# Sliding-window attention block with a SiLU feed-forward: from pool-scheduled stages to one hand-ordered stream, with projections beside attention, four-head score bursts, masks on GpSimd and reused SBUF regions

## The chip, the core and the metric

The kernel runs on one core of one Trainium2 chip. The core has TensorE (PE: matmuls and transposes, with weight loads shown apart as PEld), VectorE (DVE), ScalarE (ACT), GpSimd (POOL), SyncE (SP, which here only issues transfers) and 16 DMA engines. The metric is the device time of one execution in microseconds (us).

## What is computed

Input `x` is 2048 rows of 1024 bf16 numbers. The reference, cut to what matters:

```
def _A_ref(x, wqkv, wo):
    B, S, D = x.shape
    H = 32; Dh = D // H; W = 256
    qkv = (x @ wqkv) ...
    scores = jnp.einsum("bhqd,bhkd->bhqk", q, k) * (Dh ** -0.5)
    mask = (idx[:, None] - idx[None, :] >= 0) & (idx[:, None] - idx[None, :] < W)
    p = _softmax(jnp.where(mask[None, None], scores, -1e9), axis=-1)
    o = jnp.einsum("bhqk,bhkd->bhqd", p, v)
    return o ... @ wo
h = x + _A_ref(_layernorm(x), A_wqkv, A_wo)
h2 = h + einsum(silu(einsum(_layernorm(h), B_w1)), B_w2)      # B_w1: 1024 x 3584
```

There are 32 heads of 32 numbers. A query sees itself and the 255 rows before it, so a tile of 128 queries meets three tiles of 128 keys: its own (upper-triangular mask), the one before (no mask) and the one before that (mask on the other side).

## The kernel before

Rows are worked in 16 tiles of 128, four tiles to a block of 512 (b = 0 to 3). There are three stages, one after the other, each with its own tile pools; inside a stage a scheduler orders the instructions of each engine by dependencies and buffers.

1. Projections (lines 133 to 163). For each block: load x (L126), layernorm on DVE (statistics L45 and L46, reciprocal root by four Newton steps L28 to L31, normalization L52), transposes on PE (L143) copied out by DVE (L144), then 24 dense groups of eight 128x512 matmuls: 16 for q and k (L150), 8 for v (L159). ACT copies each group out of PSUM (L152, L162). A column of ones beside v (VW = 33) gives the softmax sums.
2. Attention (lines 184 to 238), one query tile at a time. For each pair of heads, six score matmuls (L200: 32 rows of the array, 128 columns) write `sc`; ACT takes the exponential (L207) into `eT`; DVE multiplies two of the three 128-wide pieces by masks (L209, L210); six matmuls with 33 columns (L216) add up `o_ps`; DVE divides (L221, L222). When a query tile's 32 heads are done, `o_sb` is transposed (L228, L230), projected by `wo` in 16 matmuls of 512 columns (L235, one PSUM buffer, `misc`), added to x (L237) and written to `h_dram` (L238). `w1` (7.3 MB) is loaded on POOL's queue and `wo` (2 MB) on SP's once the projections have freed their space (L170, L178); `x_t` (L187) stands behind `wo`.
3. Feed-forward (lines 254 to 284). For each block: reload h (L256), layernorm, transposes (L263, L264), 28 groups of eight matmuls with `w1` (L269), tanh on ACT (L272) and the product on DVE (L273) for SiLU, then 8 groups of 28 matmuls with `w2` (L280), residual (L282) and output (L284). `w2` (7.3 MB) is loaded on POOL's queue after the attention stage has freed its space (L246).

Of the kernel before, what the change touches and what calls it, by code (L numbers as in the profile page):

```python
# [9 lines left out]
F32 = mybir.dt.float32  # L10
# [10 lines left out]
def _rsqrt_newton(nc, pool, v_ap, out_ap, shape, tagp):  # L21
    vi = v_ap.bitcast(I32)
    yi = out_ap.bitcast(I32)
    nc.vector.tensor_scalar(out=yi, in0=vi, scalar1=1, scalar2=None, op0=ALU.logical_shift_right)
    nc.vector.tensor_scalar(out=yi, in0=yi, scalar1=-1, scalar2=0x5F3759DF, op0=ALU.mult, op1=ALU.add)
    t = pool.tile(shape, F32, name=f"rsq_t_{tagp}", tag=f"rsq_t_{tagp}")
    for _ in range(4):
        nc.vector.tensor_tensor(out=t, in0=out_ap, in1=out_ap, op=ALU.mult)  # L28
        nc.vector.tensor_tensor(out=t, in0=t, in1=v_ap, op=ALU.mult)
        nc.vector.tensor_scalar(out=t, in0=t, scalar1=-0.5, scalar2=1.5, op0=ALU.mult, op1=ALU.add)  # L30
        nc.vector.tensor_tensor(out=out_ap, in0=out_ap, in1=t, op=ALU.mult)  # L31


def _layernorm_block(nc, small, xb, ln, nj, D, tagp):
    FMAX = nc.vector.BN_STATS_FMAX
    nch = (D + FMAX - 1) // FMAX
    SD = nc.vector.BN_STATS_DIM
    AD = nc.vector.BN_AGGR_DIM
    stats = small.tile([P, nj, nch, SD], F32, name=f"ln_stats_{tagp}", tag=f"ln_stats_{tagp}")
    mv = small.tile([P, nj, AD], F32, name=f"ln_mv_{tagp}", tag=f"ln_mv_{tagp}")  # L40
    for j in range(nj):
        for c in range(nch):
            lo = c * FMAX
            hi = min(D, lo + FMAX)
            nc.vector.bn_stats(out=stats[:, j, c, :], in_=xb[:, j, lo:hi])  # L45
        nc.vector.bn_aggr(out=mv[:, j, :], in_=stats[:, j, :, :])  # L46
    var = small.tile([P, nj], F32, name=f"ln_var_{tagp}", tag=f"ln_var_{tagp}")
    nc.vector.tensor_scalar(out=var, in0=mv[:, :, 1], scalar1=LN_EPS, scalar2=None, op0=ALU.add)
    rstd = small.tile([P, nj], F32, name=f"ln_rstd_{tagp}", tag=f"ln_rstd_{tagp}")
# [9 lines left out]
def kernel(  # L59
# [15 lines left out]
    F = B_w1.shape[1]  # L75
    H = N_HEADS
    DH = D // H
    assert DH == 32 and D % P == 0 and S % 512 == 0 and F % P == 0
    NT = S // P
    KT = D // P  # L80
    FT = F // P
# [233 lines left out]
```

## Time and profile before

| what | value |
|---|---|
| timed runs | 963.44, 964.41, 967.6 us; median 964.41 |
| span of the profiled execution | 960.9 us; its own time is not given beside it, the median lies 3.5 us above the span |
| busy | PE 890.9 us (93%), DVE 370.4 (39%), ACT 311.7 (32%), POOL 13.1 (1%) |
| moved | 44.95 MB by DMA, mean 47 GB/s |
| mean granted TensorE clock | 0.865 of full |

The span is the time from the first to the last instruction on the core. The chain of work that ended last is followed back from the last instruction, at each step to what released it; an "issue" row in it is time in which an engine waited for nothing that the profile shows. Busy time on PE is occupancy: it does not say how fast the array was clocked. That stands in its own column, PEclk, 1.00 for full speed. A row of the timeline gives start, duration, engine, line, operation, output<-input, shape, count, and in brackets the idle time before it with what ended it.

### The profile page before, as it was taken

What the parts mean: (1) busy time and instruction counts of PE and PEld (TensorE: products, weight loads), DVE (VectorE), ACT (ScalarE), POOL (GpSimd) and SP (SyncE); (2) the same over time, 40 slices, a digit from 0 to 9 for tenths busy, and PEclk for the clock granted to TensorE, in tenths of its full rate; (3) what the DMA queues carried; (4) which work ended last, traced back from release to release, by engine and by line L of the source; (5) the groups of instructions that cost most, each with busy time, mean ns of one, the idle gap of its engine ahead of it and who ended that gap; (6) DMA issues with size and microseconds to landing.
All of it is one profiled execution on the core that took longest, in us unless ns stands there. A gap on an engine that the chain in (4) does not pass through costs nothing.

```text
span 960.9 us, 14267 instructions
## 1 busy us (share of the span) xinstructions
PE 890.9 (93%) x6012; PEld 448.8 (47%) x6080; DVE 370.4 (39%) x1112; ACT 311.7 (32%) x465; POOL 13.1 (1%) x26
## 2 busy tenths in 40 slices
PE   3999999968999999999999399999999999999998
PEld 2454444434555555555555144444444444444443
DVE  5940100034555545545555753215521463123311
ACT  0323333343655655555565023101310032003200
POOL 1000000010000000000000200000000000000000
PEclk9999999956766666667676689999999999999999
DMA  9200000091100000000100550001000200000000
GB/s 365 72 1 1 1 1 1 1 370 69 38 30 23 23 24 23 24 23 23 34 34 13 196 209 1 12 23 55 1 1 23 65 1 1 23 23 1 1 23 22
DMA packets 16559, 44.95 MB, mean 47 GB/s; under 512 B 1392, under 2 KB 1392, under 8 KB 16496
## 3 DMA queue, kind: packets, MB, share of 16 engines
q1 hardware_dynamic: 13440, 29.36, 8.6%
q0 software_dynamic: 3056, 14.68, 4.0%
q8 instruction: 47, 0.77, 0.3%
q14 instruction: 16, 0.13, 0.0%
HBM read 35.65 MB, written 8.39 MB: 46 GB/s over the span
## 4 chain that ended last, share of the span: by engine, by line
PE 81%; issue 8%; DVE 4%; DMA 3%; ACT 3%; SPq 0%; ACTq 0%; DVEq 0%
PE h L269 20%; PE acc L280 20%; PE sc L200 12%; PE acc L150 12%; PE o_ps L216 7%; PE acc L159 6%; PE acc_o L235 3%; ACT eT L207 3%; DMA x_t<-in_A_x_dram 2%; PE tpo L228 1%; DVE ln_stats_b L45 1%; DVE ln2T L264 1%; PE tp L143 1%; DMA x_blk<-in_A_x_dram 1%; DVE ln_stats_a L45 0%
## 5 line engine op out<-in xcount | busy, mean ns | idle before, releaser
L207 ACT ACTIVATE eT<-sc 128x768 bf16<-128x768 f32 (+2 forms) x256 | 187.6, 769 | 150.1 <-issue 65.5
L269 PE MATMUL h<-ln2T,w_sb 128*128 128x512 bf16 x876 | 194.8, 381 | 4.4 <-DVE ln2T L264 3.1
L280 PE MATMUL acc<-w_sb,gT 128*128 128x512 bf16 x880 | 193.2, 379 | 0.8
L272 ACT ACTIVATE th<-h 128x512 f32<-128x512 f32 x112 | 66.9, 597 | 311.2 <-PE h L269 304.5
L200 PE MATMUL sc<-qT_all,kT_all 32*128 32x128 bf16 x1440 | 159.9, 268 | 3.5 <-ACT eT L207 1.4
L269 PEld LDWEIGHTS <-w_sb 128*128 128x128 bf16 x896 | 88.1, 98 | 110.0 <-issue 6.2
L280 PEld LDWEIGHTS <-gT 128*128 128x128 bf16 x896 | 87.7, 98 | 105.7
L273 DVE SCALAR_TENSOR_TENSOR gT<-th,h 128x512 bf16<-128x512 f32 x112 | 76.8, 686 | 101.9 <-ACT th L272 101.8
L150 PE MATMUL acc<-lnT,wqkv_sb 128*128 128x512 bf16 x500 | 110.6, 379 | 2.5 <-DVE lnT L144 1.7
L216 PE MATMUL o_ps<-v_aug,eT 128*128 128x33 bf16 x1440 | 110.2, 192 | 1.8 <-DVE eT L209 0.6
L216 PEld LDWEIGHTS <-eT 128*128 128x128 bf16 x1440 | 72.6, 105 | 66.4 <-issue 22.9
L235 PE MATMUL acc_o<-wo_sb,oT 128*128 128x512 bf16 x240 | 85.1, 497 | 15.0 <-DMA wo_sb<-in_A_wo_dram 7.5
L210 DVE TENSOR_TENSOR eT<-eT,maskU 128x256 bf16<-128x256 bf16 x256 | 72.0, 282 | 47.9 <-ACT eT L207 47.5
L282 DVE SCALAR_TENSOR_TENSOR o_t<-acc,hb 128x512 bf16<-128x512 f32 x32 | 22.1, 692 | 168.8 <-PE acc L280 154.6
L200 PEld LDWEIGHTS <-kT_all 32*128 32x128 bf16 x1440 | 72.0, 105 | 28.6 <-issue 10.4
L209 DVE TENSOR_TENSOR eT<-eT,maskL 128x256 bf16<-128x256 bf16 x224 | 63.8, 285 | 49.7 <-ACT eT L207 48.9
L150 PEld LDWEIGHTS <-wqkv_sb 128*128 128x128 bf16 x512 | 49.8, 98 | 62.0 <-DVE lnT L144 1.6
L159 PE MATMUL acc<-wqkv_sb,lnT 128*128 128x512 bf16 x252 | 55.7, 379 | 0.2
L235 PEld LDWEIGHTS <-oT 128*128 128x128 bf16 x256 | 28.4, 120 | 55.1 <-issue 39.8
L237 DVE TENSOR_TENSOR h_t<-acc_o,x_t 128x512 bf16<-128x512 f32 x32 | 22.1, 692 | 61.7 <-PE acc_o L235 48.8
L144 DVE COPY lnT<-tp 128x1024 bf16<-128x1024 bf16 x16 | 10.2, 685 | 89.2 <-PE tp L143 89.2
L152 ACT CAST qT_all<-acc 128x512 bf16<-128x512 f32 x32 | 18.7, 586 | 64.9 <-PE acc L150 64.9
(47 smaller groups left out, 296.4 us busy)
## 6 DMA issues: line engine op xcount, KB each, us to landing
w_sb<-in_B_w_dram POOLq DMA_DIRECT2D x8, 896.0 KB, 15.1
w_sb<-in_B_w_dram POOLq DMA_DIRECT2D x7, 1024.0 KB, 11.8
wqkv_sb<-in_A_wqkv_dram SPq DMA_DIRECT2D x8, 768.0 KB, 11.1
x_blk<-in_A_x_dram SPq DMA_DIRECT2D x4, 1024.0 KB, 7.3
x_t<-in_A_x_dram SPq DMA_DIRECT2D x16, 256.0 KB, 2.8
h_dram<-h_t SPq DMA_DIRECT2D x16, 256.0 KB, 2.0
hb<-h_dram SPq DMA_DIRECT2D x4, 1024.0 KB, 5.9
out_dram<-o_t SPq DMA_DIRECT2D x16, 256.0 KB, 2.0
```

The lines of the kernel that those rows point to most:

```text
L150: nc.tensor.matmul(acc[:], lhsT=wqkv_sb[:, kt, col0:col0 + P], rhs=lnT[:, kt, :], start=(kt == 0), stop=(kt == KT - 1))
L159: nc.tensor.matmul(acc[:], lhsT=lnT[:, kt, j * P:(j + 1) * P], rhs=wqkv_sb[:, kt, col0:col0 + 512], start=(kt == 0), stop=(kt == KT - 1))
L200: nc.tensor.matmul(sc[:, hh, j * P:(j + 1) * P], lhsT=kT_all[r0:r0 + DH, g, kt * P:(kt + 1) * P], rhs=qT_all[r0:r0 + DH, g, qt * P:(qt + 1 ...
L207: nc.scalar.activation(out=eT[:, :, jlo * P:3 * P], in_=sc[:, :, jlo * P:3 * P], func=ACT.Exp, scale=scale)
L209: nc.vector.tensor_tensor(out=eT[:, :, 0:P], in0=eT[:, :, 0:P], in1=maskL_b, op=ALU.mult)
L210: nc.vector.tensor_tensor(out=eT[:, :, 2 * P:3 * P], in0=eT[:, :, 2 * P:3 * P], in1=maskU_b, op=ALU.mult)
L216: nc.tensor.matmul(o_ps[:, hl, 0:VW], lhsT=eT[:, hh, j * P:(j + 1) * P], rhs=v_aug[:, kt, h, :], start=(j == jlo), stop=(j == 2),)
L235: nc.tensor.matmul(acc[:], lhsT=oT[:, kt, :], rhs=wo_sb[:, kt, c * 512:(c + 1) * 512], start=(kt == 0), stop=(kt == KT - 1))
L269: nc.tensor.matmul(h1[:], lhsT=w1_sb[:, kt, ft * P:(ft + 1) * P], rhs=lnT[:, kt, :], start=(kt == 0), stop=(kt == KT - 1))
L272: nc.scalar.activation(out=th[:], in_=h1[:], func=ACT.Tanh, scale=0.5)
L273: nc.vector.scalar_tensor_tensor(out=gT[:, ft, :], in0=th[:], scalar=1.0, in1=h1[:], op0=ALU.add, op1=ALU.mult)
L280: nc.tensor.matmul(acc[:], lhsT=gT[:, ft, j * P:(j + 1) * P], rhs=w2_sb[:, ft, c * 512:(c + 1) * 512], start=(ft == 0), stop=(ft == FT - 1))
```

## The change

The whole program is written in one order by hand (`tc.manual_schedule()`), without pools for the large tiles: six SBUF regions are made once and viewed at fixed offsets by everything that uses them over time (`r_w` holds first wqkv, then w1; `r_t` the transposed layernorm of odd blocks, then residual tiles; `r_o` the x tiles, then wo; `r_a` q, k, v, later the gated activations, most of w2, and h of block 0; `r_e` the exponentials, later h and its transpose).

- Block 0 is projected first, tile by tile. Then, for b = 1 to 3, each of the 24 dense groups of block b follows a score burst of block b-1. The 24 bursts of block 3 stand beside the `wo` groups of blocks 0 to 2; block 3's `wo` groups stand inside the first feed-forward block.
- A burst (`scores`) covers 4 heads at once and 512 queries in three kinds A, B, C (`PIECES`): two matmuls per head, 512 columns in all, the four heads in the four row groups of the array and in four PSUM banks. Two exponentials of 128x1024 follow on ACT.
- Masks are applied in place by GpSimd's `affine_select`, not by DVE's multiplications.
- The 24 + 24 value matmuls of a head group, then its four transposes, are put behind the dense groups of the next head group's three bursts (`pending`, `tail_of`). Layernorm steps of the next block are dealt out one per burst (`steps`).
- PSUM evictions of dense groups beside attention are on DVE. 14 matmuls on zeros open the PE stream. All loads are issued by SP, w1 in 8 pieces at the end of the projections, w2 in 7 pieces into slots as they come free.

On PE, before, in the middle of the attention stage (`o_ps` values, `sc` scores, `eT` exponentials, `kT_all` keys):

```order
L216 MATMUL o_ps<-v_aug,eT 128x33
L200 LDWEIGHTS kT_all
L200 MATMUL sc<-qT_all,kT_all 128x128
L200 LDWEIGHTS kT_all
L200 MATMUL sc<-qT_all,kT_all 128x128
L216 LDWEIGHTS eT
L216 MATMUL o_ps<-v_aug,eT 128x33
```

On PE, after, the end of a dense group of block b and the value matmuls behind it (`r_w` weights, `r_t` activations, `r_e` exponentials, `r_a` v; the bracket names the engine waited for):

```order
L193 LDWEIGHTS r_t
L193 MATMUL acc_83<-r_w,r_t 128x512
L265 LDWEIGHTS r_e [waits Pool_49]
L265 MATMUL o_ps<-r_a,r_e 128x33
L265 LDWEIGHTS r_e
L265 MATMUL o_ps<-r_a,r_e 128x33
```

What moved: attention's small matmuls stood among themselves; now each run of them stands behind eight 512-column matmuls, and they wait for POOL where they waited for DVE.

On SP, before, from the end of the projections into attention (w1 is on POOL's queue):

```order
L126 DMA x_blk<-in_A_x_dram 128x4x1024 x3
L178 DMA wo_sb<-in_A_wo_dram 128x1024 x8
L187 DMA x_t<-in_A_x_dram 128x1024 x2
L238 DMA h_dram<-h_t 128x1024
L187 DMA x_t<-in_A_x_dram 128x1024
```

On SP, after, from the projections of block 3 into its attention (`in_B_w_dram` is w1; L206 is `load_res`, the residual tiles of the `wo` groups):

```order
L345 DMA r_o<-in_A_wo_dram 128x4x1024
L346 DMA r_o<-in_A_wo_dram 128x4x1024
L363 DMA r_w<-in_B_w_dram 128x3584 x8
L206 DMA r_t<-in_A_x_dram 128x1024 x2
L216 DMA h_dram<-r_t 128x1024
L206 DMA r_t<-in_A_x_dram 128x1024
```

What moved: wo is loaded a block earlier, and the first residual tiles now stand behind the eight pieces of w1 on the one queue that issues everything.

On DVE, before, in the attention stage:

```order
L237 TENSOR_TENSOR h_t<-acc_o,x_t 128x512
L209 TENSOR_TENSOR eT<-eT,maskL 128x2x128
L210 TENSOR_TENSOR eT<-eT,maskU 128x2x128
L209 TENSOR_TENSOR eT<-eT,maskL 128x2x128
L210 TENSOR_TENSOR eT<-eT,maskU 128x2x128
```

On DVE, after, where block 3's attention begins (`acc_82`, `acc_83` dense groups, L213 the addition of a residual tile):

```order
L203 CAST r_a<-acc_82 128x512
L283 COPY r_a<-tp_ps 128x512
L213 TENSOR_TENSOR r_t<-acc_83,r_t 128x512
L272 RECIPROCAL recip<-o_ps 128x8
L273 TENSOR_TENSOR r_n<-o_ps,recip 128x4x64
L213 TENSOR_TENSOR r_t<-acc_82,r_t 128x512
```

What moved: the mask products are gone from DVE and evictions of dense groups have come; the division of the previous head group stands behind the first residual addition.

The diff, cut to its core:

```diff
+PIECES = {
+    "A": [(0, 0, 3, 0), (-2, 0, 1, 3)],
+    "B": [(-1, 0, 2, 0), (2, 2, 2, 2)],
+    "C": [(3, 3, 1, 0), (1, 1, 3, 1)],
+}
+CHUNKS = [
+    [(-2, "A", 3), (-1, "B", 0), (0, "A", 0)],
+    [(-1, "B", 1), (0, "A", 1), (1, "C", 1)],
+    [(0, "A", 2), (1, "C", 2), (2, "B", 2)],
+    [(1, "C", 3), (2, "B", 3), (3, "C", 0)],
+]
+KINDS = "ABC"
...
+    h_dram = dram.tile([S, D], BF16, name="h_dram")
+    r_w = big.tile([P, 28672], BF16, name="r_w")
+    r_t = big.tile([P, 4096], BF16, name="r_t")
+    r_o = big.tile([P, 8192], BF16, name="r_o")
...
+    r_e = big.tile([P, 12288], BF16, name="r_e")
+    r_n = big.tile([P, 1536], BF16, name="r_n")
+    sc = [ps.tile([P, 2, 512], F32, name=f"sc{i}") for i in range(2)]
...
+    wqkv = view(r_w, 0, KT, 3 * D)
+    w1 = view(r_w, 0, KT, F)
+    lnT_b = [view(r_w, 24576, KT, 512), view(r_t, 0, KT, 512)]
+    x_ring = [view(r_o, i * 1024, 1024) for i in range(8)]
+    wo = view(r_o, 0, KT, D)
+    t_in = [view(r_t, i * 1024, 1024) for i in range(2)]
+    t_out = [view(r_t, 2048 + i * 1024, 1024) for i in range(2)]
+    qT = [view(r_a, (4096, 8192, 12288, 0)[b], G, 512) for b in range(NB)]
+    kT = [view(r_a, 16384 + 4096 * b, G, 512) for b in range(NB)]
+    v = view(r_a, 32768, S // P, H, VW)
+    gT = view(r_a, 4096, FT, 512)
+    W2_SLOT = (0, 1, 2, 3, 6, 4, 5)
+    w2_off = 18432
+    w2 = [view(r_a, w2_off + 4096 * s, 4, D) for s in W2_SLOT]
+    ebuf = [view(r_e, 1024 * i, 2, 512) for i in range(12)]
+    h_blk = [view(r_a, w2_off + 4096 * 4, 4, D)] + [view(r_e, 8192, 4, D)] * 3
+    ln2T = [view(r_a, w2_off + 4096 * 5, KT, 512), view(r_e, 0, KT, 512), view(r_e, 4096, KT, 512), view(r_e, 0, KT, 512)]
+    wqkv_v = A_wqkv.rearrange("(kt p) n -> p kt n", p=P)
+    wo_v = A_wo.rearrange("(kt p) n -> p kt n", p=P)
+    w1_v = B_w1.rearrange("(kt p) f -> p kt f", p=P)
+    w2_v = B_w2.rearrange("(ft p) n -> p ft n", p=P)
...
-    for b in range(NB):
-        xb = x_blks.pop(b)
-        if b + 1 < NB:
-            load_x_blk(b + 1)
-        ln = lnp.tile([P, 4, D], BF16, name="ln1", tag="ln1")
-        _layernorm_block(nc, small, xb, ln, 4, D, "a")
-        lnT = lnp.tile([P, KT, 512], BF16, name="lnT", tag="lnT")
...
-        for g in range(G):
-            for which, dst in ((0, qT_all), (1, kT_all)):
-                col0 = which * D + g * P
-                acc = psA1.tile([P, 512], F32, name="acc", tag="acc")
-                for kt in range(KT):
-                    nc.tensor.matmul(acc[:], lhsT=wqkv_sb[:, kt, col0:col0 + P], rhs=lnT[:, kt, :],
-                                     start=(kt == 0), stop=(kt == KT - 1))
-                nc.scalar.copy(out=dst[:, g, b * 512:(b + 1) * 512], in_=acc[:])
...
-    for qt in range(NT):
...
-                sc = psA2.tile([P, 2, 512], F32, name="sc", tag="sc")
...
-                eT = ework.tile([P, 2, 3 * P], BF16, name="eT", tag="eT")
-                nc.scalar.activation(out=eT[:, :, jlo * P:3 * P], in_=sc[:, :, jlo * P:3 * P], func=ACT.Exp, scale=scale)
-                if jlo == 0:
-                    nc.vector.tensor_tensor(out=eT[:, :, 0:P], in0=eT[:, :, 0:P], in1=maskL_b, op=ALU.mult)
-                nc.vector.tensor_tensor(out=eT[:, :, 2 * P:3 * P], in0=eT[:, :, 2 * P:3 * P], in1=maskU_b, op=ALU.mult)
...
+    def load_x(b, j):
+        nc.sync.dma_start(out=x_ring[(b % 2) * 4 + j], in_=x2d[(b * 4 + j) * P:(b * 4 + j + 1) * P, :])
+    def load_wqkv(c0):
+        nc.sync.dma_start(out=wqkv[:, :, c0:c0 + 512], in_=wqkv_v[:, :, c0:c0 + 512])
+    load_x(0, 0)
+    load_wqkv(2 * D)
+    load_x(0, 1)
+    load_wqkv(2 * D + 512)
+    load_x(0, 2)
+    load_x(0, 3)
+    for c0 in (0, D, 512, D + 512):
+        load_wqkv(c0)
+    make_identity(nc, ident[:])
+    warm = ebuf[0]
+    nc.vector.memset(warm, 0.0)
+    nc.gpsimd.memset(v[:, :, :, DH:VW], 1.0)
+    for i in range(14):
+        nc.tensor.matmul(sc[0][:, i % 2, :], lhsT=warm[:, 0, 0:P], rhs=warm[:, 0, :], start=True, stop=True)
...
+    def load_res(b, j, src):
+        nc.sync.dma_start(out=t_in[j % 2], in_=src[(b * 4 + j) * P:(b * 4 + j + 1) * P, :])
+    def wo_group(b, j, c):
+        acc = next_acc()
+        for g in range(G):
+            nc.tensor.matmul(acc, lhsT=qT[b][:, g, j * P:(j + 1) * P], rhs=wo[:, g, c * 512:(c + 1) * 512],
+                             start=(g == 0), stop=(g == G - 1))
+        nc.vector.tensor_tensor(out=t_out[j % 2][:, c * 512:(c + 1) * 512], in0=acc,
+                                in1=t_in[j % 2][:, c * 512:(c + 1) * 512], op=ALU.add)
+        if c == 1:
+            nc.sync.dma_start(out=h_dram[(b * 4 + j) * P:(b * 4 + j + 1) * P, :], in_=t_out[j % 2])
...
+    def scores(b, g, kind):
+        for kt, q0, nq, ch in PIECES[kind]:
+            t = b * 4 + kt
+            if t < 0:
+                continue
+            for hh in range(4):
+                r0 = hh * DH
+                nc.tensor.matmul(
+                    sc[hh // 2][:, hh % 2, ch * P:(ch + nq) * P],
+                    lhsT=kT[t // 4][r0:r0 + DH, g, (t % 4) * P:(t % 4 + 1) * P],
+                    rhs=qT[b][r0:r0 + DH, g, q0 * P:(q0 + nq) * P],
+                    start=True, stop=True, tile_position=(r0, 0),
+                )
+        lo, hi = 0, 512
...
+            e = e_of(b * G + g, kind, pair)
+            nc.scalar.activation(out=e[:, :, lo:hi], in_=sc[pair][:, :, lo:hi], func=ACT.Exp, scale=scale)
+            if kind == "A":
+                mask(e, 0, 1, True)
+                mask(e, 2, 1 if b == 0 else 2, False)
+            elif kind == "B":
+                if b > 0:
...
+    def mask(e, c0, n, upper):
+        ap = e[:, :, c0 * P:(c0 + n) * P].rearrange("p h (c q) -> p h c q", q=P)
+        sgn = 1 if upper else -1
+        nc.gpsimd.affine_select(out=ap, in_=ap, pattern=[[0, 2], [0, n], [sgn, P]],
+                                compare_op=ALU.is_ge if upper else ALU.is_gt,
+                                fill=0.0, base=0, channel_multiplier=-sgn)
...
+    def attn_out(b, g, pair):
+        i = b * G + g
+        for qt in range(4):
+            for hh in range(2):
+                chunks = [x for x in CHUNKS[qt] if b * 4 + x[0] >= 0]
+                for n, (kt, kind, ch) in enumerate(chunks):
+                    nc.tensor.matmul(
+                        o_ps[:, qt * 2 + hh, 0:VW],
+                        lhsT=e_of(i, kind, pair)[:, hh, ch * P:(ch + 1) * P],
+                        rhs=v[:, b * 4 + kt, g * 4 + pair * 2 + hh, :],
+                        start=(n == 0), stop=(n == len(chunks) - 1),
+                    )
...
+    def attn_transpose(b, g):
+        i = b * G + g
+        for qt in range(4):
+            nc.tensor.transpose(out=tp_ps[:, qt * P:(qt + 1) * P], in_=obuf[i % 3][:, qt, :], identity=ident[:])
+        nc.vector.tensor_copy(out=qT[b][:, g, :], in_=tp_ps[:, 0:512])
...
+    def tail_of(b, g):
+        return [lambda: attn_out(b, g, 0), lambda: attn_out(b, g, 1), lambda: attn_transpose(b, g)]
...
+    for b in range(1, NB):
+        dense = [lambda j=j, c=c: v_group(b, j, c, dve) for j in range(4) for c in range(2)]
+        dense += [lambda w=w, g=g: qk_group(b, w, g, dve) for g in range(G) for w in range(2)]
+        if b + 1 < NB:
+            for j in range(4):
...
+        else:
+            steps = []
+            nc.sync.dma_start(out=wo[:, 0:4, :], in_=wo_v[:, 0:4, :])
+            nc.sync.dma_start(out=wo[:, 4:8, :], in_=wo_v[:, 4:8, :])
+        n = 0
+        for g in range(G):
+            for kind in KINDS:
+                scores(b - 1, g, kind)
+                dense[n]()
+                if pending:
+                    pending.pop(0)()
+                if steps and n >= 4 and n % 3 != 2:
+                    steps.pop(0)()
+                n += 1
+            pending = tail_of(b - 1, g)
+        while steps:
+            steps.pop(0)()
...
+    for kt in range(KT):
+        nc.sync.dma_start(out=w1[:, kt, :], in_=w1_v[:, kt, :])
...
+    load_res(0, 0, x2d)
...
+    for g in range(G):
+        for kind in KINDS:
+            scores(NB - 1, g, kind)
+            b, j, c = dense[n]
...
+            wo_group(b, j, c)
+            if pending:
+                pending.pop(0)()
+            if n == 9:
+                steps = ln2_steps(0)
+                nc.sync.dma_start(out=w2[0], in_=w2_v[:, 0:4, :])
+            if steps and n >= 9:
+                steps.pop(0)()
+            n += 1
+        pending = tail_of(NB - 1, g)
+    while steps:
...
+    for b in range(NB):
+        extra = []
+        if b == 0:
+            extra = [(f, 1) for f in pending]
+            pending = []
+        for ft in range(FT):
+            acc = h1_group(b, ft)
+            if extra:
+                extra.pop(0)[0]()
+                if not extra and b == 0:
+                    for i in (1, 2, 3, 4):
+                        load_w2(i)
+            silu(b, acc, ft)
...
+        if b == 0:
+            load_w2(6)
+        steps = ln2_steps(b + 1) if b + 1 < NB else []
+        load_res(b, 0, h_dram)
...
+                nc.vector.scalar_tensor_tensor(out=t_out[j % 2][:, c * 512:(c + 1) * 512], in0=acc, scalar=0.5,
+                                               in1=t_in[j % 2][:, c * 512:(c + 1) * 512], op0=ALU.mult, op1=ALU.add)
...
+        while steps:
+            steps.pop(0)()
```

357 lines of the change are left out of this document (169 added, 188 removed).

## The prediction

> **What bounds the kernel now.** The span first, then the windows by stage, then the chain of waits.
>
> ```profile
> span 960.9 us, 14267 instructions
> ```
>
> The windows view gives busy time per engine, then PEclk, DMA share and GB/s; three windows are the middles of stages, four are looks at one place.
>
> ```profile
> 130.00:180.00 50.00, 48.85 (x235) 22.67 (x239) 1.29 (x2) 16.40 (x28) 0.00 (x0) 1.00 0.00 0
> 206.00:210.00 4.00, 2.04 (x5) 0.60 (x4) 0.57 (x2) 0.45 (x1) 0.00 (x0) 0.50 1.03 409
> 224.00:225.00 1.00, 0.64 (x16) 0.35 (x12) 0.97 (x3) 0.59 (x2) 0.00 (x0) 1.00 0.00 0
> 323.00:324.00 1.00, 1.00 (x29) 0.79 (x27) 0.53 (x1) 0.00 (x0) 0.00 (x0) 1.00 0.00 0
> 330.00:331.00 1.00, 1.00 (x16) 0.66 (x13) 0.98 (x5) 0.79 (x2) 0.00 (x0) 0.50 0.00 0
> 340.00:420.00 80.00, 76.28 (x791) 43.34 (x796) 42.43 (x158) 44.38 (x59) 0.00 (x0) 0.67 0.09 28
> 580.00:650.00 70.00, 69.63 (x319) 31.75 (x325) 15.99 (x24) 10.15 (x17) 0.00 (x0) 1.00 0.03 12
> ```
>
> Projections (130 to 180) and feed-forward (580 to 650) keep PE at full clock, without gaps. Attention (340 to 420) shows PE just as busy, at a mean clock of 0.67: 1.00 at 323, 0.50 at 330. It is the slow stage, with the two seams beside it. The chain in order of time (start, length, what) dates them:
>
> ```profile
> 56.35 5.34 PE acc L159 x24
> ...
> 197.11 22.43 DMA x_t<-in_A_x_dram
> ...
> 321.74 4.61 issue
> ...
> 343.08 5.52 issue
> ...
> 557.60 1.44 PE h L269 x3
> ...
> 660.30 10.74 PE h L269 x49
> 671.09 10.74 PE h L269 x49
> ...
> 760.52 10.74 PE h L269 x49
> ```
>
> Block 0 is projected by 61.7; the chain then waits 22.43 us for `x_t`, queued behind weights; one query tile takes 343.08 - 321.74 = 21.3 us; feed-forward starts at 557.6 and one block of it takes 100.2 us. 49 shown matmuls (one record is missing) and the next start give 10.79 / 50 = 0.216 us per dense matmul, 1.73 per group of eight; 448 of them are 96.7, so 3.5 us per feed-forward block are its layernorm seam.
>
> **Block 0, after.** The layernorm of the first block before:
>
> ```profile
> 6.11 1.88 DVE L45 BATCH_NORM_STATS2 ln_stats_a<-x_blk 128x6 f32<-128x512 bf16 x3 [6.11 <-DMA x_blk<-in_A_x_dram]
> ...
> 11.44 0.17 DVE L48 TENSOR_SCALAR ln_var_a<-ln_mv_a 128x4 f32<-128x4 f32 x1
> ...
> 15.23 1.92 DVE L52 TENSOR_SCALAR ln<-x_blk,ln_mv_a,ln_rstd_a 128x1024 bf16<-128x1024 bf16 x4
> ```
>
> A megabyte lands at 6.1; a quarter of it comes 0.75 MB / 409 GB/s = 1.9 earlier, at 4.2. One tile's layernorm: two statistics of 0.63 and the aggregate, 1.4; 15 small steps (19 took 3.79 above, 0.2 each), 3.0; normalization 0.48; so 9.1. Then each of four tiles costs PE two dense groups, 3.45, and about 1.9 for its transposes and ACT's copy behind two evictions, in which PE waits: 4 x 5.35 = 21.4, to 30.5. Sixteen q and k groups are 27.6; the next block's 32 transposes, a quarter of a dense matmul each, 1.7, and a wait on the one transpose buffer, 1. Total **61**, as before: nothing gained. The zero matmuls lie under the load.
>
> **One burst.** The terms at full clock, from the timeline:
>
> ```profile
> 217.99 1.09 ACT L207 ACTIVATE eT<-sc 128x512 bf16<-128x512 f32 x2 [11.54 <-PE sc L200]
> ```
>
> ```profile
> 224.07 0.30 PE L200 MATMUL sc<-qT_all,kT_all 32*128 32x128 bf16 x8
> ```
>
> ```profile
> 323.06 0.82 PEld L216 LDWEIGHTS <-eT 128*128 128x128 bf16 x22
> ```
>
> ```profile
> 338.02 2.27 ACT L207 ACTIVATE eT<-sc 128x768 bf16<-128x768 f32 x3 [1.23 <-PE sc L200]
> ```
>
> - Scores: eight matmuls over the four row groups stood in 0.30 us (clock 1.00 at 224), where one after another at 0.054 each they would need 0.43; so row groups run together. A burst streams 512 columns per head: 0.216 when four run together, 0.86 when none do. I take 0.3.
> - Dense group: 1.73.
> - Value matmuls: 22 weight loads in 0.82, 0.034 each (clock 1.00 at 323): 24 take 0.82. Kind C has four transposes in their place, 0.22.
> - ACT: 0.757 for 768 columns, 0.545 for 512, so 0.97 for 1024, two per burst. Behind the second, the next scores and their flight to ACT, 0.5: a floor of 2.45.
> - Changing between sorts of matmul and their semaphores: 0.15, an estimate (bounds 0 and 0.4).
>
> A and B: 0.3 + 1.73 + 0.82 + 0.15 = 3.0, PE's. C: PE needs 2.25, ACT's 2.45 decides. Mean **2.82**; 72 bursts, 203. In block 0 a query tile has fewer keys (18 value matmuls for 24): 24 bursts at 2.6, 62. Transposes of three layernorms, 5. Together **270**. It replaces the projections of blocks 1 to 3, sixteen query tiles and both seams, 61.7 to 557.6, 496 us in all, but for what stands below.
>
> DVE per three bursts: three evictions, two divisions and a transpose copy, none above 0.69 by the rows here, and 1.7 of layernorm (13.3 us a block, worked out like the first tile's, over eight head groups): under 5.9 of 8.45 us, not the bound.
>
> ```profile
> L237 DVE TENSOR_TENSOR h_t<-acc_o,x_t 128x512 bf16<-128x512 f32 x32 | 22.1, 692 | 61.7 <-PE acc_o L235 48.8
> L144 DVE COPY lnT<-tp 128x1024 bf16<-128x1024 bf16 x16 | 10.2, 685 | 89.2 <-PE tp L143 89.2
> ```
>
> POOL's timeline shows three selects and a memset, no mask of the new sizes:
>
> ```profile
> 1.19 0.28 POOL masks.py:199 TENSOR_SCALAR_AFFINE_SELECT ident<-ident 128x128 bf16<-128x128 bf16 x1
> 1.43 0.28 POOL L96 TENSOR_SCALAR_AFFINE_SELECT maskU<-maskU 128x128 bf16<-128x128 bf16 x1
> 1.67 0.20 POOL L98 MEMSET maskL<- 128x128 bf16 x1
> ...
> 3.73 0.49 POOL L99 TENSOR_SCALAR_AFFINE_SELECT maskL<-maskL 128x128 bf16<-128x128 bf16 x1
> ```
>
> A head group's masks are 12 selects over 4096 columns. Start to start, 0.24 per 128 columns: 1.9 ns a column, 7.7 us, under the 8.45 of three bursts. By the spans it is 9.1 (0.28) to 15.6 (0.49). I take 7.7, the two rows that stand undisturbed; the last select starts while another POOL instruction runs. [...]
>
> **The seam into block 3's attention.** w1's eight pieces wait for block 3's last dense groups, since they reuse `r_w`, and `load_res(0,0)` stands behind them on SP. 7.34 MB at 409 GB/s are 18, with the residual tile and landing about 20. DVE reaches the first residual addition after 2 us (scores and a dense group) and stops there, in order; the divisions of the last head group of block 2 are queued behind it, so `o_ps` stays taken. PE runs that burst, the next scores and dense group, 5 us in all, and waits at its second run of value matmuls until 21: 16. The clock falls to 0.50 in such a gap (window 206 to 210, same wait before) and costs about 2 on return. **18.** The `x_t` wait above is its like. Behind it, `hb` of block 0 lands behind 1 MB of w2: 1.
>
> **Feed-forward and end.**
>
> ```profile
> 957.20 0.69 DVE L282 SCALAR_TENSOR_TENSOR o_t<-acc,hb 128x512 bf16<-128x512 f32 x1 [5.35 <-PE acc L280]
> ```
>
> 1792 dense matmuls, 386.7; the 64 of block 3's `wo`, 13.8; value matmuls and transposes of the last head group, 2; three layernorms' transposes, 5 (their DVE work now lies under 48 us of matmuls); the last w2 piece, issued only when the first `w1` half is done, 1. **409.** After the last eviction starts, 3.7 as now.
>
> Sum: 61 + 270 + 18 + 1 + 409 + 3.7 = 762.7 of span, and 3.5 around it (964.41 - 960.9): **766 us**.
>
> **The rivals.**
>
> 1. POOL binds. At 0.28 per 128 columns and 0.2, an estimate, for each of six waits on ACT a head group takes 10.3 instead of 8.45; PE then waits at each first run of value matmuls. 24 head groups: +44, block 0 +2: 812. For it: the spans on POOL. Against it: the starts 0.24 apart. Chance 0.18.
> 2. No wait at w1: the residual tiles land among w1's pieces, or DVE's stop is covered: 748. Against it: `x_t` now, 22.43 us. Chance 0.08.
> 3. The clock falls in the bursts. One row holds full clock while dense matmuls ran:
>
> ```profile
> 324.22 1.89 PE L235 MATMUL acc_o<-wo_sb,oT 128*128 128x512 bf16 x8
> ```
>
>    They end at 326.1, and the clock is at 0.50 at 330, with PE shown fully busy by small matmuls. So small matmuls do not hold it; whether 1.73 dense us in every 2.82 do, no row shows. I think so: no stretch of 3 us is without them. At half clock a burst is 3.45 + 0.6 + 1.2 + 0.15 = 5.4, kind C 4.5, mean 5.1; 72 x 5.1 + 24 x 4.8 + 10 = 492 for 270: 988, slower than before. It needs nine in ten bursts at half clock to lose, (964 - 766) / 222. Half of them give 877. Chances 0.03 for all, 0.09 for part. [...]
>
> **How the numbers follow.** Forecast 0.60, POOL 0.18, no wait 0.08, part of the bursts slow 0.09, all slow 0.03, unnamed 0.02. The forecast's own bounds: 0.25 more or 0.15 less per burst is 24 or -14, scores one after another 0.56 x 96 = 54 at worst: 750 to 800. The range takes in no wait and POOL, 738 to 825. Within 0.5% is about what a measurement of this kernel tells from no change. Faster 0.95, same 0.01, slower 0.04.
>
> **What would show it.** Right: PEclk 1.00 through the bursts but for one gap; a burst every 2.8 us; a wait of 15 to 20 us for `r_t` by DMA at L213, with PE behind it; no "<-POOL" among PE's larger waits; feed-forward blocks of 98.5. Wrong: PE waiting for POOL at L265 in every head group (rival 1), PEclk near 0.5 beside dense groups (rival 3), PE waiting for ACT in all kinds (scores not together).

## The result, and the profile after

The changed kernel takes 845.37 us, the median of four runs (844.29 to 846.42), beside 966.0 for the kernel before (963.44 to 967.65): a ratio of 0.876, 95% interval 0.8737 to 0.8783. The forecast was 766 us, so the sign is right, but the time is 79 us above the forecast and lies above the range (738 to 825) too. The profiled execution took 846.29 us. The first lines of the profile's page give the span, the busy time of each engine and the row of the granted clock over the span:

```profile
span 844.6 us, 12753 instructions
...
PE 724.2 (86%) x5265; PEld 353.4 (42%) x5358; DVE 329.5 (39%) x738; ACT 257.1 (30%) x325; POOL 171.6 (20%) x375
...
PEclk9999999999996989999999999999999999999999
```

PE is now at full clock nearly everywhere, but busy for 86% of the span instead of 93%: time is lost in gaps, not to the clock. Three rows of the timeline date the stages: the first score burst, the first feed-forward group, the last eviction.

```profile
60.12 0.34 PE L229 MATMUL sc<-r_a 32*128 32x384 bf16 x4
...
347.40 1.89 PE L402 MATMUL acc<-r_a,r_w 128*128 128x512 bf16 x8
...
841.03 0.69 DVE L446 SCALAR_TENSOR_TENSOR r_t<-sc,r_t 128x512 bf16<-128x512 f32 x1 [5.35 <-PE sc L444]
```

Set beside the terms of the sum (all us; bursts are 270 with the w1 seam's 18 and 1 for `hb`):

| stage | predicted | after |
|---|---|---|
| block 0's projections | 61 | 60.1 |
| 96 bursts with the seam | 289 | 287.3 |
| feed-forward to the last eviction | 409 | 493.6 |
| end | 3.7 | 3.6 |
| around the span | 3.5 | 1.7 |

Everything ahead of the feed-forward came as forecast, and the feed-forward is 85 us too long. (The term around the span was 1.8 too large: 964.41 was set against the span of another execution, and in the runs that have both, time and span differ by 1.7.) Before, PE ran the feed-forward almost without a gap (69.63 of 70 us busy). The windows view (PE, PEld, DVE, ACT, POOL busy, then PEclk, DMA share, GB/s) shows where PE now stands idle, first in the bursts, then at the seam, then in one feed-forward block:

```profile
61.00:250.00 189.00, 183.47 (x2189) 101.34 (x2222) 107.52 (x253) 126.87 (x142) 121.44 (x267) 1.00 0.04 13
250.00:272.00 22.00, 7.43 (x84) 3.81 (x82) 1.92 (x5) 5.82 (x6) 6.28 (x14) 0.74 0.89 357
...
485.00:608.00 123.00, 102.28 (x473) 46.28 (x483) 37.86 (x72) 16.72 (x28) 0.00 (x0) 0.99 0.08 26
```

The bursts keep PE busy for 97% at clock 1.00. The feed-forward window has the clock too, 0.99, and yet PE is idle for 20.7 of its 123 us. The list of PE's waits (waiting instruction, what it waited for: us in total, times, longest) names them:

```profile
PE sc L402 <- DVE r_a L412: 47.4, 33, 1.5
PE o_ps L265 <- DVE r_n L273: 18.6, 2, 16.6
PE sc L444 <- DVE r_t L446: 13.3, 8, 3.2
...
PE sc L402 <- DVE r_t L213: 4.9, 6, 1.0
...
PE acc L211 <- DVE r_t L213: 4.3, 1, 4.3
...
PE sc L402 <- DVE r_t L446: 2.4, 3, 0.8
```

The second row is the w1 seam. In the first, third, fourth and last, matmuls that write `sc` in the feed-forward wait for DVE. The timeline of one such wait:

```profile
489.47 0.60 ACT L411 ACTIVATE r_a<-sc 128x512 f32<-128x512 f32 x1 [1.13 <-PE sc L402]
490.10 0.69 DVE L412 SCALAR_TENSOR_TENSOR r_a<-r_a,sc 128x512 bf16<-128x512 f32 x1 [1.04 <-ACT r_a L411]
490.84 1.89 PE L402 MATMUL sc<-r_e,r_w 128*128 128x512 bf16 x8 [1.41 <-DVE r_a L412]
```

A group ends in one bank of `sc` at 489.4 (a bank is here the 128x512 f32 numbers that one group writes). Before the next group may start in the other bank, tanh (0.60) and the product (0.69) of the group just finished have to be through: PE stands for 1.41 us. In the feed-forward the banks follow one another as `acc0`, `acc1`, then the first and second half of `sc0`, then those of `sc1`. The second half of each waits; that is two waits in six groups. The chain shows what six groups then take:

```profile
485.80 3.64 PE sc L402 x16
...
499.31 3.63 PE sc L402 x16
```

13.51 us, where six groups without a wait would be 6 x 1.73 = 10.4 (10.36 in e1, below). Half of 13.51 - 10.36 is 1.58: so much a wait costs, 0.17 more than its idle time.

### The profile page after: what moved, and what is told of

Its sections match the earlier page's. It is cut to its first block, busy times and chain, and to the rows that moved or that the text cites. A ratio compares the mean times of both kernels' runs of the same rounds, so it can differ in the third digit from the quotient of the medians.

```text
span 844.6 us, 12753 instructions
## 1 busy us (share of the span) xinstructions
PE 724.2 (86%) x5265; PEld 353.4 (42%) x5358; DVE 329.5 (39%) x738; ACT 257.1 (30%) x325; POOL 171.6 (20%) x375
## 4 chain that ended last, share of the span: by engine, by line
PE 77%; DVE 10%; DMA 8%; ACT 3%; issue 2%; SPq 0%; ACTq 0%; DVEq 0%
PE sc L402 15%; PE sc L444 13%; PE acc L201 12%; PE acc L444 8%; PE acc L402 7%; PE acc L193 7%; PE acc L211 4%; PE o_ps L265 4%; PE sc L229 3%; DMA r_t<-in_A_x_dram 3%; DVE r_a L412 3%; DMA r_e<-h_dram 2%; ACT r_a L411 2%; DVE r_t L446 2%; PE tp_ps L173 1%
## 5 line engine op out<-in xcount | busy, mean ns | idle before, releaser
L240 ACT ACTIVATE r_e<-sc 128x1024 bf16<-128x1024 f32 (+2 forms) x192 | 175.8, 967 | 112.7 <-PE sc L229 112.7
L255 POOL TENSOR_SCALAR_AFFINE_SELECT r_e<-r_e 128x256 bf16<-128x256 bf16 (+1 forms) x368 | 168.6, 487 | 176.4 <-ACT r_e L240 172.5
L402 PEld LDWEIGHTS <-r_w 128*128 128x128 bf16 x896 | 87.1, 97 | 166.3 <-issue 65.0
L402 PE MATMUL sc<-r_e,r_w 128*128 128x512 bf16 x452 | 105.0, 379 | 41.4 <-DVE r_a L412 38.8
L444 PEld LDWEIGHTS <-r_a 128*128 128x128 bf16 x896 | 88.1, 99 | 121.9 <-issue 20.5
L444 PE MATMUL sc<-r_a 128*128 128x512 bf16 x548 | 125.9, 386 | 13.9 <-DVE r_t L446 13.3
L444 PE MATMUL acc<-r_a 128*128 128x512 bf16 x327 | 73.7, 379 | 1.0 <-DMA r_a<-in_B_w_dram 0.6
L201 PEld LDWEIGHTS <-r_w 128*128 128x128 bf16 x512 | 46.1, 98 | 59.4 <-issue 10.3
L265 PE MATMUL o_ps<-r_a,r_e 128*128 128x33 bf16 x1440 | 46.4, 178 | 18.6 <-DVE r_n L273 18.6
L201 PE MATMUL acc<-r_t,r_w 128*128 128x512 bf16 x240 | 58.0, 380 | 3.0 <-issue 1.7
L265 PEld LDWEIGHTS <-r_e 128*128 128x128 bf16 x1440 | 45.9, 96 | 34.3 <-issue 19.7
L201 PE MATMUL acc<-r_w 128*128 128x512 bf16 x244 | 57.0, 379 | 1.7 <-issue 0.9
L211 PE MATMUL acc<-r_o,r_a 128*128 128x512 bf16 x195 | 51.5, 404 | 5.9 <-DVE r_t L213 4.3
L412 DVE SCALAR_TENSOR_TENSOR r_a<-r_n,sc 128x512 bf16<-128x512 f32 x30 | 20.6, 688 | 78.3 <-ACT r_n L411 78.3
L402 PE MATMUL acc<-r_e,r_w 128*128 128x512 bf16 x208 | 48.6, 379 | 0.4
L402 PE MATMUL sc<-r_a,r_w 128*128 128x512 bf16 x139 | 33.4, 378 | 13.7 <-DVE r_a L412 8.6
L229 PE MATMUL sc<-r_a 32*128 32x128 bf16 (+2 forms) x704 | 40.5, 279 | 0.0
L211 PEld LDWEIGHTS <-r_a 128*128 128x128 bf16 x256 | 24.0, 101 | 36.9 <-issue 14.2
L213 DVE TENSOR_TENSOR r_t<-acc,r_t 128x512 bf16<-128x512 f32 x26 | 17.8, 685 | 45.1 <-PE acc L211 25.3
```

What stands on the lines that cost most here:

```text
L201: nc.tensor.matmul(acc, lhsT=wqkv[:, kt, col0:col0 + P], rhs=lnT_b[b % 2][:, kt, :], start=(kt == 0), stop=(kt == KT - 1))
L211: nc.tensor.matmul(acc, lhsT=qT[b][:, g, j * P:(j + 1) * P], rhs=wo[:, g, c * 512:(c + 1) * 512], start=(g == 0), stop=(g == G - 1))
L229: nc.tensor.matmul(sc[hh // 2][:, hh % 2, ch * P:(ch + nq) * P], lhsT=kT[t // 4][r0:r0 + DH, g, (t % 4) * P:(t % 4 + 1) * P], rhs=qT[b][r0 ...
L240: nc.scalar.activation(out=e[:, :, lo:hi], in_=sc[pair][:, :, lo:hi], func=ACT.Exp, scale=scale)
L255: nc.gpsimd.affine_select(out=ap, in_=ap, pattern=[[0, 2], [0, n], [sgn, P]], compare_op=ALU.is_ge if upper else ALU.is_gt, fill=0.0, base ...
L265: nc.tensor.matmul(o_ps[:, qt * 2 + hh, 0:VW], lhsT=e_of(i, kind, pair)[:, hh, ch * P:(ch + 1) * P], rhs=v[:, b * 4 + kt, g * 4 + pair * 2 ...
```

## The experiments

Theory: `sc0` and `sc1` are each declared as one tile of two banks, and the program's dependencies go by tile. A matmul that begins in the second half is held until the last reader of the first half is done, though the two are different banks. Rivals: the feed-forward needs more than six banks or more buffers for tanh, and its round trip through ACT and DVE is simply the pace; or two neighbouring banks of PSUM disturb one another in the chip. Other runs test the terms that came out right, since they might have done so by accident. Times are medians; each ratio is to the kernel before, with its 95% interval.

**e1_bank_order: the two halves kept three groups apart.**

```diff
-    acc_banks += [sc[i][:, j, :] for i in range(2) for j in range(2)]
+    acc_banks[:] = [acc_ps[0][:], sc[0][:, 0, :], sc[1][:, 0, :], acc_ps[1][:], sc[0][:, 1, :], sc[1][:, 1, :]]
```

> Only the order of the six PSUM banks in the feed-forward stage changes: the two halves of one score tile are used three groups apart, not one after the other. Theory (a tile of two banks is waited for as a whole: a group on its second half waits until ACT and DVE are done with the group on its first half): the 47 us that PE waits at L402 for DVE's products go, three groups no longer lose 1.58 us each time a tile's halves follow each other; a feed-forward block falls from 121.8 us to about 105, total about 776. Rival (PE waits because ACT's tanh and DVE's product with two th buffers are too slow for six banks in turn): as many banks, as many buffers, so 845 as before.

767.19 us (766.12 to 767.81), ratio 0.7948 [0.7931, 0.7966]: 78.2 below the changed kernel. In its chain six groups lie between these two rows:

```profile
476.01 3.45 PE sc L402 x16
...
486.37 3.45 PE sc L402 x16
```

They take 10.36 us. No wait for L412 is left in the list of PE's waits, and the time is 9 below the 776 expected. These are the same six banks in another order: they were never too few.

**e2_two_banks: the feed-forward on `acc0` and `acc1` alone.**

```diff
-    acc_banks += [sc[i][:, j, :] for i in range(2) for j in range(2)]
```

> The feed-forward stage uses only the two single-bank PSUM tiles acc0 and acc1, not six banks. Theory (halves of one tile): the product of a group ends 1.5 us after its last matmul and the next group takes 1.73, so two banks of two tiles are enough: about 780, faster than with six. Rival (banks or buffers are short): fewer banks make it slower than 845.

768.22 us (766.95 to 769.77), ratio 0.7961 [0.7941, 0.7981]. Four banks fewer are 77 us faster, again more than expected. The four banks that the change added to the rotation brought nothing but the wait.

**e9_three_th: a third buffer for tanh.**

```diff
-    th_first = [r_e[:, 1024 * i:1024 * (i + 1)].bitcast(F32) for i in range(2)]
+    th_first = [r_e[:, 1024 * i:1024 * (i + 1)].bitcast(F32) for i in range(3)]
...
-        th = (th_first if b == 0 else th_later)[ft % 2]
+        th = (th_first if b == 0 else th_later)[ft % 3]
```

> Three th buffers for tanh instead of two; the bank order is as in the changed kernel. Theory (halves of one tile): 845, within 2 us. Rival (buffers of tanh): the 47 us of waits at L402 go, about 785.

845.52 us (843.61 to 847.11), ratio 0.876 [0.8736, 0.8784], no change. Its list of PE's waits begins as that of the changed kernel:

```profile
PE sc L402 <- DVE r_a L412: 47.3, 33, 1.5
```

The buffers of tanh are not what PE waits for.

**e11_split_tiles: the same order of banks, declared as four tiles.** e1 and e2 leave open whether the tile or the neighbourhood of two banks makes the wait. Here the order stays, and only the declaration changes.

```diff
...
+    sc_pool.__exit__(None, None, None)
+    ff_ps = ctx.enter_context(tc.tile_pool(name="ps_ff", bufs=1, space=bass.MemoryType.PSUM))
-    acc_banks += [sc[i][:, j, :] for i in range(2) for j in range(2)]
+    acc_banks += [ff_ps.tile([P, 512], F32, name=f"ff{i}")[:] for i in range(4)]
```

> The feed-forward's four extra banks are declared as four tiles of one bank each, opened where the two score tiles of two banks end; the order of the banks (two accumulators, then the four, neighbours one after the other) is that of the changed kernel. Theory, the two halves of a two-bank tile are one object for the program's dependencies, so that the second half's first matmul waits for the product on the first half: with separate tiles no such wait is written, the row for the wait at L402 for the product at L412 goes, and the time is that of the other bank order, 767 us (765 to 772). Rival, the wait comes of two neighbouring banks being written and read one after the other, whatever the tiles are: 845 us, and the row stays at about 47 us.

In the kernel the score tiles stand in a pool of their own, declared behind the other PSUM tiles; this pool ends and the four tiles are made in its place. 768.4 us (766.88 to 769.85), ratio 0.796 [0.7938, 0.7982]. The first rows of its list of PE's waits (lines lie two lower in this kernel):

```profile
PE o_ps L267 <- DVE r_n L275: 19.1, 2, 16.4
PE tp_ps L175 <- DVE r_e L176: 5.6, 6, 0.9
```

The seam is now the first, and the waits of 47 and 13 us are gone. So the wait is written into the program by the declaration of the tile; it is not a property of the banks. (The trace doesn't show where in PSUM a tile lies; that the four are neighbours is inferred from their being declared one behind the other in the place that the score tiles leave.)

**e3_w1_dealt: w1's pieces behind the residual tiles.** One piece is issued in every second burst, instead of all eight ahead of the first residual tile.

```diff
-    for kt in range(KT):
-        nc.sync.dma_start(out=w1[:, kt, :], in_=w1_v[:, kt, :])
...
+            if n < 16 and n % 2 == 0:
+                nc.sync.dma_start(out=w1[:, n // 2, :], in_=w1_v[:, n // 2, :])
             wo_group(b, j, c)
```

> The eight pieces of w1 are issued one every second burst of block 3's attention, behind the first residual tile, not all ahead of it. Theory (the residual tile is queued behind 7.3 MB, DVE stops at the addition, PE behind it): the 16.6 us that PE waits at L265 for DVE's division go, and the low clock after it: about 827. Rival (the wait only moves to later residual tiles, which now stand behind single pieces): 835 to 845.

826.65 us (825.42 to 829.61), ratio 0.8561 [0.8539, 0.8583], 18.7 below the changed kernel. The wait of 16.6 us at L265 is no longer among its rows. The seam's price, forecast at 18, is what its removal returned.

**e4_masks_dve: the masks back on DVE**, as 16 multiplications of 256 columns per head group, in the new order of the stream.

```diff
...
-        nc.gpsimd.affine_select(out=ap, in_=ap, pattern=[[0, 2], [0, n], [sgn, P]],
...
+        for c in range(c0, c0 + n):
+            ap = e[:, :, c * P:(c + 1) * P]
+            m = (maskU if upper else maskL)[:].unsqueeze(1).to_broadcast([P, 2, P])
+            nc.vector.tensor_tensor(out=ap, in0=ap, in1=m, op=ALU.mult)
```

> One part of the change undone: masks are DVE multiplications of 256 columns again, 16 per head group, the rest is the changed kernel. Theory (GpSimd takes off DVE what DVE has no room for in a burst): at 0.285 us each they are 4.6 us beside the 3.7 that evictions, divisions and the copy take, with layernorm over the 8.0 us of three bursts; PE waits for DVE in the score bursts, total 860 to 890. Rival (DVE was 39% busy, so the masks cost nothing there): 845 within 5.

856.77 us (855.82 to 857.33), ratio 0.8878 [0.886, 0.8896]: 11.4 above the changed kernel, in the direction expected but below the range expected. The window of the bursts and two waits:

```profile
61.00:250.00 189.00, 179.44 (x2116) 97.84 (x2149) 169.44 (x578) 122.42 (x137) 0.00 (x0) 1.00 0.04 13
```

```profile
PE o_ps L270 <- DVE r_n L278: 22.1, 7, 15.9
...
PE o_ps L270 <- DVE r_e L262: 6.5, 3, 5.3
```

DVE is busy for 169 of 189 us, 90%, instead of 107.5. The two rows together count ten waits and 28.6 us. Two of these waits, 18.6 us, the changed kernel has too, the w1 seam above all; the eight others and their 10 us are nearly the whole difference, and everywhere else DVE keeps pace. Moving the masks to POOL is worth 11 us here, a small part of the change.

**e5_apart: bursts without dense groups between them.** The dense groups of blocks 1 to 3 run ahead of the attention of blocks 0 to 2. The work is the same.

```diff
+        for n in range(24):
+            dense[n]()
...
             for kind in KINDS:
                 scores(b - 1, g, kind)
-                dense[n]()
```

> One part of the change undone: the dense groups of blocks 1 to 3 all run ahead of the attention of blocks 0 to 2, not beside it; block 3's attention is as in the changed kernel. Theory (a burst alone is bound by two exponentials and the way between PE and ACT, about 2.45, and PE's dense groups hide nothing when they stand alone): 72 times 2.45 + 1.73 - 2.66, +109: 955; the clock in the bursts alone falls to 0.50 and adds up to 15. Rival (the gain lies in the bursts and the masks, not in what stands beside them): 860 or less.

935.9 us (934.1 to 937.17), ratio 0.9697 [0.9674, 0.972]: 90.5 above the changed kernel. This is less than the 955 expected and far above the rival's 860. A window of bursts alone, the largest wait, and ACT's exponentials there, two for each burst:

```profile
250.00:330.00 80.00, 53.01 (x787) 29.13 (x786) 17.13 (x51) 59.76 (x63) 57.77 (x124) 0.50 0.01 1
```

```profile
PE sc L229 <- ACT r_e L240: 51.9, 117, 1.1
```

```profile
290.70 1.94 ACT L240 ACTIVATE r_e<-sc 128x1024 bf16<-128x1024 f32 x2 [0.69 <-PE sc L229]
293.22 1.94 ACT L240 ACTIVATE r_e<-sc 128x1024 bf16<-128x1024 f32 x2 [0.58 <-POOL r_e L255]
295.85 1.94 ACT L240 ACTIVATE r_e<-sc 128x1024 bf16<-128x1024 f32 x2 [0.69 <-PE sc L229]
298.47 1.94 ACT L240 ACTIVATE r_e<-sc 128x1024 bf16<-128x1024 f32 x2 [0.69 <-PE sc L229]
```

Bursts alone are granted half the clock for 80 us on end, and PE waits for ACT in them, at 117 places. Beside dense groups the same bursts had 1.00 for 189 us, in the row above. So the dense groups do two things for the bursts: they hold the clock, and they fill the time of the exponentials. How the two share is an estimate from the rows. Three bursts alone take 298.47 - 290.70 = 7.77 us, 2.59 each, of which 1.94 are the exponentials; at full clock, in the changed kernel, ACT stood 0.53 between two pairs (the row at 205.04 below), which would make 2.47. The low clock then costs a burst alone 0.12, some 9 us in 72 bursts, and the rest is cover. What a low clock would cost with the dense groups beside the bursts, the run doesn't show.

The undoing also removes the w1 seam, since w1 is loaded here behind the last dense group, under the bursts alone: the window 200 to 201 of this run shows the DMA at 437 GB/s, and the first seven rows of its list of PE's waits, down to 3.9 us, have none at L265, where the changed kernel has 18.6. With the 18.7 that e3 gives for the seam, the dense groups beside 72 bursts are worth about 109 us, an estimate, as expected. That is about half of what projections and attention gained (496 us before by the prediction's dates, 287 after); what the four heads of a burst and the rest contribute to the other half, no run parts.

Idle gaps between groups that cycle through PSUM banks did not bring the clock down: the feed-forward after has such gaps, two of 1.4 us in every 13.5, between groups of 1.73 us, and its window of 123 us shows 0.99.

**e10_head_by_head: the score matmuls of a burst head by head**, not piece by piece over the four row groups.

```diff
-        for kt, q0, nq, ch in PIECES[kind]:
-            t = b * 4 + kt
...
-            for hh in range(4):
+        for hh in range(4):
+            for kt, q0, nq, ch in PIECES[kind]:
+                t = b * 4 + kt
...
```

> One part of the change undone: in a score burst each head's two matmuls follow each other, head by head, in place of one matmul of each of the four heads in turn. Same matmuls, same outputs. Theory (row groups run together when neighbours in the stream are on different ones): a burst's scores rise from about 0.35 to 0.7 or 0.8 us, in A and B in full, in C behind ACT in part: +25 to +40, 870 to 885. Rival (the array takes the heads together in either order, or the exponentials cover it): 845 within 5.

846.28 us (842.47 to 848.95), ratio 0.8767 [0.8736, 0.8798]: no change, and my theory falls. A burst with 384 columns to a matmul in the two kernels, the changed one first: the scores, and the next dense group's first weight load.

```profile
204.45 0.51 PE L229 MATMUL sc<-r_a 32*128 32x384 bf16 x8
204.88 1.41 PEld L193 LDWEIGHTS <-r_t 128*128 128x128 bf16 x8 [0.21 <-issue]
```

```profile
205.24 0.51 PE L229 MATMUL sc<-r_a 32*128 32x384 bf16 x8
205.68 1.41 PEld L193 LDWEIGHTS <-r_t 128*128 128x128 bf16 x8 [0.21 <-issue]
```

It is 0.43 and 0.44 us from the first score to the next group. One after another, four heads of 512 columns would need 0.86, an estimate, at the pace of a dense matmul (0.216). So the heads run together in either order. Why they do so when a head's own matmuls follow one another, the trace doesn't tell.

**e8_all: what the others point to, together.** The bank order of e1, w1 dealt out as in e3; besides, h of the next block is loaded at the 17th group, not behind the 28th; the last steps of its layernorm come one per group; the last w2 piece is put where block 3's q stood, so that it is issued earlier; and h of block 0 goes ahead of the first w2 piece, its statistics two bursts later. The diff is that of e1 and e3 and

```diff
+    w2[6] = view(r_a, 0, 4, D)
...
+            if ft == 16 and b == 0:
+                load_w2(6)
+            if ft == 16 and b + 1 < NB:
+                steps = ln2_steps(b + 1)
+                steps.pop(0)()
...
-                for _ in range(2):
+                for _ in range(2 if len(steps) > 3 else 1):
```

> The bank order of the feed-forward stage and the dealt pieces of w1 together, and besides: h of the next block is loaded in the middle of the w1 half, not where DVE needs it; one transpose step per group at the end of layernorm; the last piece of w2 goes to the place of block 3's q; block 0's h is loaded ahead of the first piece of w2 and its statistics start two bursts later. Theory: 767 less 18.5 for w1, less 4 to 6 for the transposes and the seam in block 3's attention, less about 1 for w2: 742. Rival (the waits for h and the transposes lie beside other work): 748.

743.23 us (741.43 to 745.05), ratio 0.7696 [0.7675, 0.7716]: the fastest of all, 102 below the changed kernel and 1 from the 742 expected. Its stages, by the rows that date them (feed-forward at L404 and L450 here):

```profile
63.00 0.34 PE L230 MATMUL sc<-r_a 32*128 32x384 bf16 x4
...
328.74 1.89 PE L404 MATMUL sc<-r_a,r_w 128*128 128x512 bf16 x8 [0.88 <-DVE r_a L175]
...
739.62 0.69 DVE L450 SCALAR_TENSOR_TENSOR r_t<-sc,r_t 128x512 bf16<-128x512 f32 x1 [5.35 <-PE sc L448]
```

The bursts without the seam take 265.7 us, the feed-forward 410.9. A feed-forward window of it has PE busy for 98.7%:

```profile
485.00:608.00 123.00, 121.43 (x578) 56.33 (x589) 47.32 (x90) 19.70 (x33) 0.00 (x0) 1.00 0.10 31
```

## Why the prediction was wrong, point by point

**The step that failed** is the first of "Feed-forward and end": "1792 dense matmuls, 386.7". It took the pace of before, 0.216 a matmul without a gap, for the changed kernel too. I read that pace from a stage with its own PSUM buffers. I did not ask which buffers the changed stage has, and none of the rivals named a wait there: what happened fell under "unnamed", 0.02. The change puts four half tiles into the rotation, two by two behind one another, and makes every third group wait: of 112 with `w1`, 32 with `w2` and 8 with `wo`, 152 in all, that is 50.7. The rows of matmuls into `sc` that wait for DVE count 33 + 8 + 6 + 3 = 50 waits and 47.4 + 13.3 + 4.9 + 2.4 = 68.0 us; with 0.17 more for each, as measured at L402, they cost 76.5 of the 78.2 us that e1 recovers. Of the signs named, this is the one that failed: a feed-forward block was to take 98.5 and takes 121.8 (485.80 to 607.63 in the chain); in e1 it takes 100.7 (470.83 to 571.50 in its chain). That the halves' common tile is the cause is shown by e1, e2 and e11; e9 excludes the buffers.

With that wait removed, and nothing else changed, the sum holds. The rows that date the stages in e1:

```profile
61.73 0.34 PE L229 MATMUL sc<-r_a 32*128 32x384 bf16 x4
...
347.34 1.89 PE L402 MATMUL sc<-r_a,r_w 128*128 128x512 bf16 x8
...
761.99 0.69 DVE L446 SCALAR_TENSOR_TENSOR r_t<-sc,r_t 128x512 bf16<-128x512 f32 x1 [5.35 <-PE sc L444]
```

61.7, 285.6, 414.7 and 3.5 us to the end of its span of 765.5: predicted 61, 289, 409 and 3.7. No term is off by more than 6. That e1's 767.19 comes within 2 us of 766 is in part luck: the bursts were 3 shorter and the feed-forward 6 longer than forecast.

**The bursts** held. The rows of three bursts on end, with ACT's first two pairs of exponentials:

```profile
202.06 0.40 PE L229 MATMUL sc<-r_a 32*128 32x128 bf16 x8
...
202.57 1.94 ACT L240 ACTIVATE r_e<-sc 128x1024 bf16<-128x1024 f32 x2 [0.82 <-PE sc L229]
...
204.45 0.51 PE L229 MATMUL sc<-r_a 32*128 32x384 bf16 x8
...
205.04 1.94 ACT L240 ACTIVATE r_e<-sc 128x1024 bf16<-128x1024 f32 x2 [0.53 <-PE sc L229]
...
207.32 0.40 PE L229 MATMUL sc<-r_a 32*128 32x256 bf16 x8
...
210.08 0.40 PE L229 MATMUL sc<-r_a 32*128 32x128 bf16 x8
```

2.39, 2.87 and 2.76 us, 8.02 for a head group where 8.45 was forecast. The last two are PE's, as argued. The first, the kind with transposes, was to be set by ACT at 2.45; that is not shown. ACT's pairs do start 2.47 apart, but ACT stands 0.53 of that waiting for the scores, and the list of PE's waits has no row in which L229 waits for ACT. The working left the 0.15 for changes between matmuls, which the other kinds carry, out of PE's 2.25 for this kind; with it PE's side is 2.40, against 2.39 measured. No run shows the 0.15 itself, an estimate without a row; the list of PE's waits from 61 to 343 has 30 idle times before dense groups put down to issue, 4.8 us in all, 0.16 each. The two limits lie within 0.1 of one another, and which of them sets this kind stays open. The scores' 0.3, the term with the widest bounds, came out as 0.43 in the kind that begins with 384 columns and 0.33 in the others (from the first score to the next dense group).

**Rival 1, POOL binds,** falls. The two sorts of selects in the groups by form:

```profile
L255 POOL TENSOR_SCALAR_AFFINE_SELECT r_e<-r_e 128x256 bf16<-128x256 bf16 x256 | 104.8, 421 | 105.1 <-ACT r_e L240 101.2
L255 POOL TENSOR_SCALAR_AFFINE_SELECT r_e<-r_e 128x512 bf16<-128x512 bf16 x112 | 71.3, 637 | 71.3 <-ACT r_e L240 71.3
```

A full head group has eight of the first and four of the second, 8 x 0.421 + 4 x 0.637 = 5.9 us where I took 7.7; 8.02 was to be had, and the list of PE's waits has no row for POOL. The difference of the two forms is 0.84 ns a column, with 0.2 us per instruction on top (spans on POOL are rough). The starts of the small 128x128 selects, 0.24 apart, had been read as if all of that grew with the columns. The 0.2 that the rival adds for each wait on ACT was an estimate without a row.

**Rival 2, no wait at w1,** falls: the seam came as described, at the second run of value matmuls, in the chain of the changed kernel:

```profile
250.91 6.00 DMA r_w<-in_B_w_dram
256.97 15.88 DMA r_t<-in_A_x_dram
...
298.76 9.22 DMA r_a<-h_dram
```

```profile
DVE r_t L213 <- DMA r_t<-in_A_x_dram: 19.9, 2, 19.5
```

DVE stops for 19.5 us at the first residual addition, and PE for 16.6 behind it, with the clock at 0.74 in that window (250 to 272); e3 returned 18.7. The third row of the chain is `hb` of block 0 behind w2: priced at 1, it held PE for 4.3 at L211 (list of waits, above). Seam, `hb` and the block's first transposes together are 287.3 - 265.7 = 21.6 by e8, for 19 in the sum.

**Rival 3, the clock,** falls for the bursts of blocks 0 to 2, at 1.00 (61 to 250). In block 3's attention, 272 to 347, the windows view gives a mean of 0.89, with the low stretches behind the two waits: 0.50 from 272 to 277 and 0.55 from 310 to 316. Without these waits, in e8, the clock is 0.98 from 250 to 330. So the waits lowered it, not the bursts, and e5 shows what the rival feared, without the dense groups: 0.50 for 80 us. The rival's price was loose, though: its 1.2 for the value matmuls at half clock comes from no row shown, and e5 has 0.86 for 24 of them (at 290.61).

**The range** (738 to 825) was drawn from the doubts about the bursts, where the forecast was good. It gave the feed-forward, more than half of the time, no bounds at all. One of its sums is off as well: 766 and the 54 for scores one after another are 820, not 800.

## What to carry to other kernels

When a change puts buffers into a rotation, write down for each the declared object that it is part of, and the last reader of that object's other parts: two views of one tile were one buffer to the dependencies here (845.37 us, for 768.4 with four tiles in e11), and six banks so declared were slower than two (768.22 in e2). A stage that runs without a gap before is not a constant of the sum if the change touches what it writes to. The small matmuls and exponentials of the bursts gained twice from the dense groups between them, by the clock (1.00 for 0.50 in e5) and by the cover (PE busy for 183.47 of 189 us, for 53.01 of 80); by the estimate under e5 the cover is the larger part for bursts that would stand alone.

## What the runs showed of the hardware that was not expected

- The order of score matmuls over the row groups of the array made no difference: 0.43 us for a burst piece by piece, 0.44 head by head (e10), each half of the 0.86 that the same columns would need one after another, an estimate at 0.216 a dense matmul.
- Gaps of 1.4 us twice in 13.5 us left the granted clock at 0.99 (feed-forward after), while bursts alone, with PE shown busy for 53 of 80 us, had 0.50 throughout (e5).
- A select on POOL took 421 ns for 256 columns and 637 ns for 512, for 128 partitions of bf16 numbers (L255 after): by their difference 0.84 ns a column, with 0.2 us on top, an estimate from the two.
- Two PSUM banks for dense groups of 1.73 us were as good as six: 768.22 (766.95 to 769.77) and 767.19 us (766.12 to 767.81).
